# A kernel whose input test is counted at the head of its last part, read back before the last outputs, and followed directly by the block for the usual case

## The chip, the core and the metric

The program runs on one core of one Trainium2 chip. Five engines work side by side, each through its own instructions in order: TensorE (PE, with its weight loads as PEld), VectorE (DVE), ScalarE (ACT), GpSimd (POOL) and SyncE (SP), which issues all transfers here. They wait for one another through semaphores. The metric is the device time of one execution in microseconds, as a median of several runs; lower is better.

## The reference, cut to what matters

Three stages follow one another: a gated linear attention, a dense layer with a leaky activation, and a soft mixture of experts.

```python
for t in range(S):                                   # B 4, H 8, S 768, D 48
    state = alpha[:, :, t, :, None] * state + k_t outer v_t
    y[:, :, t] = q_t @ state
h = x @ w_in                                         # 3072x384 @ 384x2048
g = max(h, 0) + moe_alpha * min(h, 0)
x2 = g @ w_out                                       # 3072x2048 @ 2048x384
logits = x2 @ phi                                    # 32 slots, 4 for each of 8 experts
slot_input = softmax(logits, over tokens).T @ x2     # 32x384
slot_out[e] = max(slot_input[e] @ w1[e], 0) @ w2[e]  # 384 -> 1024 -> 384
out = softmax(logits, over slots) @ slot_out         # 3072x384
```

## The kernel before

Attention works in chunks of 128 steps and divides by products of alpha, which is safe only where alpha lies between 0.75 and 1.25; the activation is computed as a maximum of two values, which holds only where `moe_alpha` is at most 1. So the kernel carries two paths. The fast path computes everything under these assumptions and writes the output. Beside it, it keeps `flags` (a tile of 128x4x8 numbers) that tell how far alpha left its bounds. `count_ok` (L503) turns them into a count of the places where the assumptions held, `values_load` (L516) reads that count into a register of every engine, and `tc.If(ok < N_OK)` (L759) runs `general_path`, which recomputes everything step by step, if the count falls short. On the inputs timed here the assumptions hold, and the general path never runs; its instructions nevertheless stand in the program.

Each engine carries out the branch for itself. The program is laid out in blocks: the main block with the fast path, ending in the test; then the block for flags that failed (the general path); then a short block for flags that held; then the end block. The short block brings the semaphores to the values that the other block would have left: PE, DVE, ACT and POOL each wait there for their own semaphore, and SP waits for its eight transfer semaphores, so for the landing of all outputs. The end block joins the engines in two barriers.

The order of the work is written out by hand in strings: each letter is a step that issues its instructions on all engines. `START`, `STEADY` and `LAST` order attention, dense layer and token softmax; `TAIL` (L630) orders what comes after them, the part that the change touches. In it `a` transposes the sums over all tokens (`ut` on PE from `acc`, L528, then ACT's copy `uT`, L532), `b` makes the slots' inputs (`si`, L539, `sT`, L544), `c` to `f` are the first expert layer (`h`, L553), `g` to `j` its transposes, `k` to `n` the second layer (`o`, L574), `o` to `r` gather the experts' results (ACT's copy `os`, L581, and PE's `so`, L582), and `s` to `z` make the output in eight parts of 576 KB (PE L599, copies on ACT L602 and DVE L604, the transfer on SP L606). `F` loads an expert weight and `C` turns combine weights. `count_ok` is called after the whole tail.

Of the kernel before, what the change touches and what calls it, by code (L numbers as in the profile page):

```python
# [9 lines left out]
I32 = mybir.dt.int32  # L10
# [12 lines left out]
N_OK = 128 * 32  # L23
# [6 lines left out]
class Kern:  # L30
# [472 lines left out]
    def count_ok(self):  # L503
        nc = self.nc
        nc.vector.tensor_scalar(out=self.flags[:, 2:4].rearrange("p a b -> p (a b)"), in0=self.alp, scalar1=1.0, scalar2=0.0, op0=ALU.subtract, op1=ALU.max)
        ok = self.sp.tile([128, 4, NSTEP], F32, tag="ok", name="ok", bufs=1)
        nc.vector.tensor_scalar(out=ok, in0=self.flags, scalar1=0.0, scalar2=None, op0=ALU.is_le)
        oks = self.sp.tile([128, 1], F32, tag="oks", name="oks", bufs=1)
        nc.vector.reduce_sum(out=oks, in_=ok.rearrange("p a b -> p (a b)"), axis=AX.X)
        ones = self.sp.tile([128, 1], F32, tag="ones", name="ones", bufs=1)  # L510
        nc.vector.memset(ones, 1.0)
        ps = self.psa("okp")[:1, :1]
        nc.tensor.matmul(ps, oks, ones, start=True, stop=True)
        n = self.sp.tile([1, 1], I32, tag="okn", name="okn", bufs=1)
        nc.vector.tensor_copy(out=n, in_=ps)
        return nc.values_load(n, min_val=0, max_val=N_OK)  # L516

    def tail_steps(self):
        nc, sp, wt = self.nc, self.sp, self.wt
# [96 lines left out]

    def tail(self):
        steps = self.tail_steps()
        for c in TAIL:
            steps[c]()  # L620
        assert not self.queue


# [3 lines left out]
START = "lplpAxpplxABwxCpxypBpAyxlBAEpCppyDJyCBCzppyDAzFzDEJEzpGdzHCIFDpGKEHFFhGMILxOwDFGxHEhHBFhDHMgGIxgJNBIhJgHKMhLKJIhKgLxxyPyhNLhgJLNgKMNOhhLOghNhgMPyyglPPpzzypOzgNgphPhpgzgPOgphpzhg"  # L627
STEADY = "hhggsgxslhsxghhxsxgxgyhhpghhhgyysgpgpgypyzzhhhphzzsgggzgphwhg"
LAST = "hQggsxhRxxshhsTxSysggxfghsyghQzzyWhQgTyhgSyzhQQRghzRShhgUVfRghgzhThghcfggsgfShhgRWTUUhsgUhXsTgUhhgVfhVWVfWggfgVfhfghhWfXgXhgsXhXghggffhsfhfshcfgscfggSgfffsfcsfscffssfcs"
TAIL = "abFCcFdgehFfCFikFjomqFlFFvstunprxwzy"  # L630
W_ORDER = ([("w1", 4 * q + e, hf) for q in range(2) for hf in range(2) for e in range(4)]
           + [("w2", e, ch) for ch in range(2) for e in range(8)])

# [11 lines left out]
def streams(k):  # L645
    def loads():
        for c in range(3):
            k.att_load(0, ("al", "k", "q", "v"), c)
            yield
        for i in range(1, NSTEP):  # L650
            k.att_load(i, ("al", "k", "q"))
            yield

    def v_loads():
        for i in range(1, NSTEP):
            k.att_load(i, ("v",))
            yield

    def pres():
        yield from k.pre_first()  # L660
        for i in range(1, NSTEP):
            yield from k.pre_gen(i)

    def atts(c):
        for i in range(NSTEP):
            yield from k.att_chunk(i, c)

    def small():
        k.small_loads()
        yield  # L670

    def repeat(f):
        while True:
            f()
            yield

    s = {"l": loads(), "w": v_loads(), "p": pres(), "x": atts(0), "y": atts(1), "z": atts(2), "d": small(),
         "h": repeat(k.h_step), "g": repeat(k.g_step), "s": k.softs(), "f": repeat(lambda: k.feed(1)), "c": repeat(k.combine_step)}
    s.update((name, k.conv_gen(*CONV[n])) for n, name in enumerate(CONV_NAMES))
    return s  # L680


def fast_path(ctx, tc, nslots, **a):
    k = Kern(ctx, tc, a, nslots)
    k.consts()
    k.moe_init()
    s = streams(k)
    for c in START + STEADY * (NSTEP - 3) + LAST:
        next(s[c])
    k.tail()  # L690
    return k.count_ok()


def general_path(tc, nslots, ys, **a):
# [41 lines left out]
    with ExitStack() as ctx:  # L736
# [5 lines left out]
        for i in range(NSTEP):  # L742
            k.x_load(i, ys)
            k.moe_run(i)
        for _ in range(NSTEP - TAIL.count("C")):
            k.combine_step()
        k.feed(len(W_ORDER) - TAIL.count("F"))
        k.tail()


def emit(tc, nslots=26, **a):
    nc = tc.nc
    with ExitStack() as outer:
        dram = outer.enter_context(tc.tile_pool(name="ys", bufs=1, space=bass.MemoryType.DRAM))
        ys = dram.tile([768, 16, 2, 48], F32, name="ys")
        with ExitStack() as ctx:
            with tc.manual_schedule():
                ok = fast_path(ctx, tc, nslots, **a)
        with tc.If(ok < N_OK):  # L759
            general_path(tc, nslots, ys, **a)  # L760


# [53 lines left out]
```

## Time and profile before

| | |
|---|---|
| median of 3 timed runs | 542.34 us (541.62 to 544.48) |
| profiled execution, first to last instruction (span) | 540.6 us |
| PE busy | 456.7 us, 84% of the span |
| DVE busy | 411.5 us, 76% |
| ACT busy / POOL busy | 224.8 us / 139.2 us |
| mean granted TensorE clock | 0.952 |

No own time is given for the profiled execution beside its span; the median of the timed runs stands 1.7 us above it. Most of the span is dense-layer work on PE. The change lies in the last 55 us, so the reader should look at three stretches there: around 486 us, where the tail begins; around 521 us, between the two halves of the output; and from 527.7 us, where the last output copy ends, to 540.6 us.

### The profile page before, as it was taken

The page shows a single profiled execution, that of the slowest core. Times are in us where ns is not written, and L with a number is a line of the kernel's source. Part 1 is how long each engine was busy: PE and PEld are TensorE (multiplying, and loading weights), DVE is VectorE, ACT ScalarE, POOL GpSimd, SP SyncE. Part 2 cuts the span into 40 slices and gives each one's busy share as a digit, 9 for nine tenths or more (in the row PEclk, how much of TensorE's full clock was granted, in tenths as well). Part 3 has the DMA queues.
Part 4 walks back from the last instruction along what each step waited for, and adds up shares of the span by engine and source line. Part 5 has one row for each costly group of instructions (what it writes and reads, how often), then busy time and mean ns, then how long its engine had stood idle before and what let it go on. Part 6 is the DMA issues. An engine that isn't in the chain of part 4 may idle for free.

```text
span 540.6 us, 10837 instructions
## 1 busy us (share of the span) xinstructions
PE 456.7 (84%) x4316; PEld 360.1 (67%) x4316; DVE 411.5 (76%) x791; ACT 224.8 (42%) x420; POOL 139.2 (26%) x75
## 2 busy tenths in 40 slices
PE   3643588789799899989998997999899999978980
PEld 2431477777688678768786886787667887653570
DVE  6999999999577976987697789769777897662140
ACT  2755345664254334324524432443236366342140
POOL 1247575875200400220030004002202263320000
PEclk9997787899899999989999999999899999989995
DMA  8994111041202436425461724454464588989955
GB/s 298 420 403 181 58 59 59 15 162 61 116 1 52 127 74 219 96 82 117 180 172 37 246 55 133 96 198 118 140 201 188 132 329 279 373 343 389 383 193 169
DMA packets 42236, 93.99 MB, mean 174 GB/s; under 512 B 5056, under 2 KB 29888, under 8 KB 42176
## 3 DMA queue, kind: packets, MB, share of 16 engines
q1 hardware_dynamic: 42176, 93.20, 51.1%
q8 instruction: 36, 0.59, 0.4%
q14 instruction: 24, 0.20, 0.1%
HBM read 69.59 MB, written 4.72 MB: 137 GB/s over the span
## 4 chain that ended last, share of the span: by engine, by line
PE 47%; DVE 41%; ACT 5%; issue 4%; DMA 1%; SPq 0%; DVEq 0%; ACTq 0%
PE h L325 25%; DVE P L191 4%; DVE tmp L235 3%; DVE g L335 3%; PE lg L370 3%; DVE st L355 3%; DVE al L199 3%; DVE w_in L106 3%; DVE w_t L106 3%; PE sc L220 2%; DVE S L255 2%; PE o L574 2%; PE h L553 2%; DVE w_t L105 2%; ACT P L147 2%
## 5 line engine op out<-in xcount | busy, mean ns | idle before, releaser
L325 PE MATMUL h<-xh,wi 128*128 128x384 f32 x768 | 223.4, 358 | 16.0 <-ACT xh L499 9.8
L325 PEld LDWEIGHTS h<-xh,wi 128*128 128x128 f32 x768 | 146.2, 196 | 30.2 <-ACT xh L499 11.3
L325 PE MATMUL h<-xl,wi 128*128 128x384 f32 x384 | 134.1, 349 | 12.1 <-DVE xl L500 12.1
L334 ACT ACTIVATE tn<-h,alp 128x384 f32<-128x384 f32 x128 | 73.6, 581 | 128.6 <-PE h L325 112.5
L335 DVE TENSOR_TENSOR g<-h,tn 128x384 f32<-128x384 f32 x128 | 68.2, 549 | 65.7 <-ACT tn L334 61.8
L325 PEld LDWEIGHTS h<-xl,wi 128*128 128x128 f32 x384 | 75.4, 196 | 14.7 <-DVE xl L500 13.9
L193 POOL TENSOR_TENSOR q<-q,P 128x1536 f32<-128x1536 f32 x7 | 24.8, 3543 | 199.0 <-DMA gT<-st 113.2
L355 DVE STREAM_TRANSPOSE st<-g 128x192 f32<-128x192 f32 x192 | 57.0, 346 | 0.3
L220 PE MATMUL sc<-q,k 48*128 48x128 f32 x384 | 35.0, 316 | 0.0
L220 PEld LDWEIGHTS sc<-q,k 48*128 48x128 f32 x384 | 27.5, 209 | 9.0 <-issue 8.4
L268 PE MATMUL y<-tmp,v 128*32 128x128 f32 x384 | 23.2, 299 | 11.0 <-DVE tmp L235 8.1
L259 ACT COPY S<-S 64x256 f32<-64x256 f32 x20 | 8.1, 406 | 54.9 <-DVE S L255 49.8
L235 DVE TENSOR_TENSOR tmp<-sc,cst 128x512 f32<-128x512 f32 x48 | 30.6, 678 | 0.2
L370 PE MATMUL lg<-g,wpr 128*32 128x384 f32 x256 | 29.0, 506 | 0.0
L111 POOL TENSOR_TENSOR raw_w_out<-raw_w_out 128x768 f32<-128x768 f32 x8 | 12.4, 1556 | 54.8 <-PE y L281 34.1
L199 DVE TENSOR_TENSOR_SCAN al<-al,Z 128x1536 f32<-128x1536 f32 x7 | 24.7, 3530 | 0.2
L191 DVE TENSOR_TENSOR_SCAN P<-al,Z 128x1536 f32<-128x1536 f32 x7 | 24.7, 3526 | 0.0
L226 PE MATMUL kt<-cst,k 128*128 128x128 f32 x80 | 15.4, 323 | 10.1 <-DVE k L171 8.7
L268 PEld LDWEIGHTS y<-tmp,v 128*32 128x32 f32 x384 | 10.3, 113 | 20.2 <-DVE tmp L235 9.3
L348 PE MATMUL tr<-cst,g 128*128 128x128 f32 x96 | 16.2, 283 | 8.7 <-DVE g L335 6.5
L203 POOL TENSOR_TENSOR k<-k,al 128x1536 f32<-128x1536 f32 x6 | 17.4, 2907 | 22.1 <-issue 14.8
L111 POOL TENSOR_TENSOR raw_w_in<-raw_w_in 128x768 f32<-128x768 f32 x8 | 14.1, 1766 | 32.6 <-DVE raw_w_in L107 27.0
(150 smaller groups left out, 721.1 us busy)
## 6 DMA issues: line engine op xcount, KB each, us to landing
w<-w SPq DMA_DIRECT2D x32, 768.0 KB, 8.4
gT<-st SPq DMA_DIRECT2D x192, 96.0 KB, 2.2
raw_w_in<-w_in SPq DMA_DIRECT2D x8, 768.0 KB, 8.4
raw_w_t<-w_t SPq DMA_DIRECT2D x8, 768.0 KB, 9.6
raw_w_out<-w_out SPq DMA_DIRECT2D x8, 768.0 KB, 5.9
v<-vT SPq DMA_DIRECT2D x7, 768.0 KB, 4.5
al<-alT SPq DMA_DIRECT2D x7, 768.0 KB, 4.5
k<-kT SPq DMA_DIRECT2D x7, 768.0 KB, 5.9
```

Of the source, the lines that this page charges most:

```text
L106: nc.vector.scalar_tensor_tensor(out=Ai, in0=pi, scalar=-0x80000000, in1=Ai, op0=ALU.bitwise_and, op1=ALU.bitwise_or)
L111: nc.gpsimd.tensor_tensor(out=B, in0=B, in1=p, op=ALU.mult)
L191: nc.vector.tensor_tensor_scan(P, al[:, 0:W6], Z, 0.0, ALU.mult, ALU.add)
L199: nc.vector.tensor_tensor_scan(G[:, ::-1], G[:, ::-1], Z[:, ::-1], 0.0, ALU.mult, ALU.add)
L220: nc.tensor.matmul(sc[h][:, p], K[r, p, c], Q[r, p, c], start=True, stop=True)
L235: nc.vector.tensor_tensor(out=m, in0=sc[h], in1=self.tri[:, None, :].to_broadcast([128, NP, 128]), op=ALU.mult)
L268: nc.tensor.matmul(y[32 * g:32 * g + 32, kt], V[:, c, p, 0, h, :], sm[h][:, p], start=True, stop=(S is None))
L325: nc.tensor.matmul(h, w[ft // 2][:, kt, fs], x[:, kt], start=(n == 0), stop=(n == 8))
L334: nc.scalar.activation(out=t, in_=h, func=AF.Copy, scale=al)
L335: nc.vector.tensor_tensor(out=g, in0=h, in1=t, op=ALU.max)
L355: nc.vector.transpose(out=self.stage[z].rearrange("p t a f j -> p (t a) f j")[:, :, f], in_=g4[:, :, z])
L370: nc.tensor.matmul(self.lg[32 * jj:32 * jj + 32], self.wpr[:, 4 * fb + jj], self.g[4 * fb + jj], start=(fb == 0), stop=(fb == 3))
```

## The change

`count_ok` no longer returns a value: it leaves its count in a tile, and a second function `read_ok` reads it into the registers. Both become steps of the tail, `1` as its first and `2` between `p` and `r`, five steps from the end. `tc.If` is told that the block for the failed flags is not the one to follow the test, so the short block for flags that held stands directly behind it.

```diff
         ps = self.psa("okp")[:1, :1]
         nc.tensor.matmul(ps, oks, ones, start=True, stop=True)
-        n = self.sp.tile([1, 1], I32, tag="okn", name="okn", bufs=1)
-        nc.vector.tensor_copy(out=n, in_=ps)
-        return nc.values_load(n, min_val=0, max_val=N_OK)
+        self.okn = self.sp.tile([1, 1], I32, tag="okn", name="okn", bufs=1)
+        nc.vector.tensor_copy(out=self.okn, in_=ps)
+
+    def read_ok(self):
+        self.ok = self.nc.values_load(self.okn, min_val=0, max_val=N_OK)
...
         steps = self.tail_steps()
+        if not self.general:
+            steps.update({"1": self.count_ok, "2": self.read_ok})
         for c in TAIL:
-            steps[c]()
+            if c in steps:
+                steps[c]()
...
-TAIL = "abFCcFdgehFfCFikFjomqFlFFvstunprxwzy"
+TAIL = "1abFCcFdgehFfCFikFjomqFlFFvstunp2rxwzy"
...
     k.tail()
-    return k.count_ok()
+    return k.ok
...
-        with tc.If(ok < N_OK):
+        with tc.If(ok < N_OK, preferred_fallthrough_block=False):
```

Three places show what this moves. The first is PE's queue at the head of the tail; names are out<-in, and the brackets name the engines whose semaphores the instruction waits for. Before:

```order
L462 MATMUL ct<-cst,cr 128x128 [waits DVE_49,Pool_49]
L462 MATMUL ct<-cst,cr 128x128 x2
L528 MATMUL ut<-cst,acc 128x128 [waits DVE_49]
L528 MATMUL ut<-cst,acc 128x128 x3
L539 MATMUL si<-w_out_4217,uT 32x384 [waits DVE_49,Activation_49]
```

PE's queue at the same place in the changed kernel (its lines stand two further on):

```order
L462 MATMUL ct<-cst,cr 128x128 [waits DVE_49,Pool_49]
L462 MATMUL ct<-cst,cr 128x128 x2
L513 MATMUL okp<-ones,oks 1x1 [waits DVE_49,PE_49]
L530 MATMUL ut<-cst,acc 128x128 [waits Activation_49]
L530 MATMUL ut<-cst,acc 128x128 x3
```

The count's matmul now stands ahead of the transposes `ut`. What it waits for is DVE's `oks` and `ones`, whose place in DVE's queue in the changed kernel is this:

```order
L441 SCALAR_TENSOR_TENSOR acc<-acc,sc,u 128x512 [waits PE_49]
L465 TENSOR_TENSOR cs_4978<-ct,cs_4978 64x384 [waits Activation_49]
L444 TENSOR_REDUCE cd<-ce 128x3
L445 TENSOR_SCALAR cd<-cd 128x3 [waits DVE_49]
L446 RECIPROCAL cd<-cd 128x3 [waits DVE_49]
L447 TENSOR_TENSOR c<-ce,cd 128x96 [waits DVE_49]
L505 TENSOR_SCALAR flags<-alp 128x16
L507 TENSOR_SCALAR ok<-flags 128x32 [waits DVE_49]
L509 TENSOR_REDUCE oks<-ok 128x1 [waits DVE_49]
L511 MEMSET ones 128x1
L515 CAST okn<-okp 1x1 [waits PE_49]
```

Before, `rd` (L524) stood directly behind `c`, and the last five of these rows stood at the very end of the queue. Between `acc`, which `ut` reads, and `ones`, which PE now awaits first, stand eight instructions.

The second place is PE's queue between the two gathers, in the changed kernel:

```order
L576 MATMUL o_5425<-w_6_1_5365,ht_5238 32x192
L576 MATMUL o_5425<-w_7_1_5367,ht_5238 32x192
L584 MATMUL so<-os,reps 128x192 [waits Activation_49]
L518 TENSOR_LOAD okn [waits DVE_49]
L584 MATMUL so<-os,reps 128x192 [waits Activation_49]
L601 MATMUL o<-ss,cs_4470 128x192 [waits DVE_49,Activation_49]
```

The register read moved from the end of the queue to between the two `so` matmuls; on the other engines it lies in the corresponding place.

The third is SP's queue at the end of the tail. Before:

```order
L606 DMA out<-ot_2_5400 128x6x192 [waits DMAHW7_49,DVE_49,Activation_49]
L606 DMA out<-ot_1_5458 128x6x192 [waits DMAHW0_49,DVE_49,Activation_49]
L606 DMA out<-ot_0_5472 128x6x192 [waits DMAHW1_49,DVE_49,Activation_49]
L606 DMA out<-ot_3_5486 128x6x192 [waits DMAHW2_49,DVE_49,Activation_49]
L606 DMA out<-ot_2_5500 128x6x192 [waits DMAHW3_49,DVE_49,Activation_49]
L516 TENSOR_LOAD okn [waits DVE_49]
L516 ISA x2
L759 COMPARE_AND_BRANCH
```

SP's queue at the end of the tail in the changed kernel:

```order
L608 DMA out<-ot_2_5411 128x6x192 [waits DMAHW7_49,DVE_49,Activation_49]
L518 TENSOR_LOAD okn [waits DVE_49]
L518 ISA x2
L608 DMA out<-ot_1_5483 128x6x192 [waits DMAHW0_49,DVE_49,Activation_49]
L608 DMA out<-ot_0_5497 128x6x192 [waits DMAHW1_49,DVE_49,Activation_49]
L608 DMA out<-ot_3_5511 128x6x192 [waits DMAHW2_49,DVE_49,Activation_49]
L608 DMA out<-ot_2_5525 128x6x192 [waits DMAHW3_49,DVE_49,Activation_49]
L764 COMPARE_AND_BRANCH
L764 UNCONDITIONAL_BRANCH [waits DMAHW0_49,DMAHW1_49,DMAHW2_49,DMAHW3_49,DMAHW4_49,DMAHW5_49,DMAHW6_49,DMAHW7_49]
```

The last row stands for the short block: its eight waits and its branch to the end block. Before, it was the last row of SP's whole queue, 785 rows behind the test and next to the end block; now it follows the test, and the 784 rows of the other block lie between it and the end block. The same holds on the other engines.

## Rows read from the trace of the kernel before

**Rows 1.** The page: span, and code fetches (packets, MB, share).

```profile
span 540.6 us, 10837 instructions
...
q8 instruction: 36, 0.59, 0.4%
q14 instruction: 24, 0.20, 0.1%
```

**Rows 2.** Chain of waits, head of the tail: start us, us, what.

```profile
486.16 0.76 DVE acc L441
...
486.96 0.67 PE ut L528 x4
...
488.29 2.83 PE si L539 x32
```

**Rows 3.** Timeline of PE around 486 us: start us, us, what.

```profile
486.03 0.55 PE L462 MATMUL ct<-cst,cr 128*128 128x128 f32 x3
```

**Rows 4.** Chain of waits from 500 us to the end, by line.

```profile
by line: PE o L574 24.4%; PE h L553 9.8%; PE o L599 8.9%; DVE ot L604 5.3%; PE so L582 4.8%; PE hTp L564 3.6%; issue 1.8%; PE ct L462 1.1%; DVE ss L587 1.0%; ACT os L581 0.7%; ACT ss L585 0.7%; PE okp L513 0.5%; DVE ok L507 0.4%; DVE oks L5
```

**Rows 5.** Timeline of DVE around 488 us.

```profile
488.59 0.14 DVE L524 TENSOR_SCALAR rd<-den 128x1 f32<-128x1 f32 x1
```

**Rows 6.** Timeline from 514 us: second gather, count ([idle before <-releaser]).

```profile
521.85 0.32 ACT L581 COPY os<-o 128x192 f32<-128x192 f32 x1 [2.35 <-PE o L574]
...
523.25 0.73 DVE L587 TENSOR_TENSOR ss<-so,ss 32x192 fp32r<-32x192 f32 x2 [3.59 <-ACT ss L585]
...
527.74 0.17 DVE L505 TENSOR_SCALAR flags<-alp 128x16 f32<-128x16 f32 x1
...
528.42 0.19 PE L513 MATMUL okp<-ones,oks 128*1 128x1 f32 x2 [1.39 <-DVE ones L511]
```

**Rows 7.** By stretch: busy PE, PEld, DVE, ACT, POOL; granted clock, DMA share, GB/s.

```profile
478.50:481.90 3.40, 0.81 (x15) 0.63 (x19) 2.46 (x8) 1.60 (x5) 0.00 (x0) 1.00 1.02 416
482.00:485.30 3.30, 3.30 (x72) 3.30 (x65) 1.77 (x8) 0.28 (x1) 0.00 (x0) 0.50 0.72 268
485.40:488.70 3.30, 2.24 (x39) 1.38 (x35) 2.19 (x7) 1.06 (x2) 0.00 (x0) 1.00 0.81 290
```

**Rows 8.** Line L516, the register read: durations in ns, first and last start.

```profile
L516 PEldq TENSOR_LOAD <-okn x1: 1167/1167/1167, 528.8 to 528.8; - x1
```

**Rows 9.** Line L462: PE's sequencer reaches the transpose `ct`.

```profile
L462 PEldq EVENT_SEMAPHORE  x2: 51/51/51, 485.1 to 491.8; - x2
```

**Rows 10.** Line L606: output transfers, issue to landing, min/median/max.

```profile
L606 SPq DMA_DIRECT2D out<-ot x8: 372/732/1435, 517.5 to 528.1; - x8
...
DMA to landing us min/median/max: 3.3/5.2/7.3
```

**Rows 11.** Line L759: the test, then the short block.

```profile
L759 SPq EVENT_SEMAPHORE  x8: 17/17/17, 537.2 to 537.7; - x8
L759 ACTq COMPARE_BRANCH  x1: 50/50/50, 530.0 to 530.0; - x1
...
L759 PEldq COMPARE_BRANCH  x1: 6582/6582/6582, 530.1 to 530.1; - x1
...
L759 ACTq EVENT_SEMAPHORE  x1: 17/17/17, 537.1 to 537.1; - x1
```

**Rows 12.** Busy and transfers by stretch at the end.

```profile
533.50:534.00 0.50, 0.00 (x0) 0.00 (x0) 0.00 (x0) 0.00 (x0) 0.00 (x0) 0.50 0.91 293
...
537.50:538.00 0.50, 0.00 (x0) 0.00 (x0) 0.00 (x0) 0.00 (x0) 0.00 (x0) 0.50 0.36 98
```

**Rows 13.** Line L813: the end block.

```profile
L813 SPq EVENT_SEMAPHORE  x10: 17/28/28, 537.8 to 540.5; - x10
...
L813 ACTq DRAIN  x2: 8/32/56, 537.2 to 540.3; - x2
...
L813 DVEq EVENT_SEMAPHORE  x2: 21/21/21, 538.5 to 540.5; - x2
...
L813 ACTq EVENT_SEMAPHORE  x2: 17/17/17, 540.2 to 540.5; - x2
```

## The prediction

> **What bounds the kernel now.** I read the page first [rows 1], then the chain of waits around the tail's head and from 500 us on [rows 2, 4], then the timelines of single engines there [rows 3, 5, 6], and last the lines of the test and of the end block [rows 11, 13], because nothing computes in the last 12 us. The reader is to see three things.
>
> At the head, PE and the engines beside it form one chain: `acc` on DVE ends at 486.9, `ut` follows at 486.96, and `si` at 488.29 [rows 2]. From 500 us on the chain is nearly all matmuls and their copies; no transfer appears in what the row shows [rows 4]. So whatever comes late at 487 us comes late at the last output copy, which ends at about 527.7, where `flags` begins [rows 6].
>
> Then come transfers. The last output is issued at 528.1 and lands up to 7.3 us later, at 535.4 [rows 10]. The outputs still move 293 GB/s just before 534 us [rows 12].
>
> Then comes code. ACT's test stands at 530.0 and takes 0.05 us, but its next instruction, in the short block, starts only at 537.1; PE's test is recorded as 6.58 us long [rows 11]. The jump goes past the whole other block, and its code arrives only when the outputs have left. The same is to be seen once more: ACT's `DRAIN` is at 537.2 and its next wait at 540.2, though DVE passes the same barrier at 538.5 [rows 13]. Meanwhile 98 GB/s for 0.5 us, 49 KB, move [rows 12]; fetches are 16.4 KB each on one queue (0.59 MB in 36) and 8.3 KB on the other [rows 1], so this is about one 16.4 KB fetch and four of 8.3 KB, five engines. A fetch with nothing in its way therefore costs about 3.0 us from need to resumption.
>
> **The change part by part.**
>
> *The count at the head.* PE works in order, so `ut` now waits behind `okp`, and `okp` for DVE's `ones`. DVE reaches `flags` where `rd` began, 488.59 [rows 5]; from `flags` to `okp` it took 527.74 to 528.42, 0.68 us [rows 6]. So `okp` starts at 489.27 and `ut` about 0.06 later, at 489.33, against 486.96 [rows 3]: +2.4 us. Behind it on PE stands the entire tail, and ACT (`uT`), then DVE and SP wait for that. Bounds: above 2.6, with all of `okp`'s 0.19 added; below 0, if a later wait took it up, for which the chain has no candidate [rows 4], so I take 2.4. The weight loads are no cover, since they are not what the tail waits for [rows 4]. The CAST behind `okp` delays `rd`, which `sis` needs some 3 us later and so doesn't feel.
>
> *The clock.* PE ends `ct` at 486.58 [rows 3] and would now idle until 489.3. [...]
>
> *The read moved.* It takes 1.17 us on PE [rows 8]. On ACT it stands where the engine idles 2.35 us, and on DVE 3.59 [rows 6], so it costs nothing there, nor on POOL, which has finished its work, nor on SP, whose next transfer waits for DVE's copies behind `ss`. On PE it is hidden if the sequencer runs ahead of the array: it passed the wait of `ct` at 485.1 [rows 9], 0.9 us before the matmul at 486.03 [rows 3]. Read that way it would start 0.9 before the second gather, and `so` awaits ACT's `os`, which ends at 522.17 [rows 6]. Bounds: 0 to 1.2; I take 0, nearest to the 0.9. If that cover went, it would cost up to the whole 1.2.
>
> *The ending.* What falls away at the end (five DVE operations, the read, the jump to the short block) lay beside the landing outputs. What matters is what comes after the landing. SP now passes the test without a jump, and waits in the short block for its outputs. On the clock of before: landing 535.4; four more semaphores at 0.07 (eight took 537.2 to 537.7 [rows 11]), 0.3; then the jump past the other block, 3.0; then the end block, from SP's first wait at 537.8 to the barrier passed at 538.5 [rows 13], 0.7, and to the end without ACT's late arrival another 0.6, an estimate. Sum 540.0 against 540.6: -0.6. If the five fetches no longer share the engines with the last output, it lands when the stream runs dry, at about 534.5, and it is -1.5. I take -0.8, close to the measured landing; the bounds are -1.5 and, with the ending as long as before, 0.
>
> [...]
>
> *Sum:* +2.4 + 1.0 + 0 - 0.8 = +2.6 us on the span of 540.6, so 543.2. The timed median stands 1.7 us above that span, and I carry this over: 542.3 + 2.6 = 544.9 us, 0.5% more at the most. Changes under 0.5%, 2.7 us, can't be told from none here (the bounds are 539.6 and 545.1), so the forecast is "no change", close to its upper edge.
>
> **The rivals.**
>
> *PE holds its queue at the read* until the matmuls before it have drained. Place: between the two `so`. Then it starts at 522.3 instead of about 521.0 and `so` waits 1.2 us longer: 546.1, slower. It decides from the moment when the read starts later than 521.0 on the clock of before. The wait passed 0.9 us ahead speaks against [rows 9]; no row shows a read with work queued before it.
>
> *The ending gives nothing back.* ACT's code arrives only when the outputs have left, as before [rows 12], and the end block costs it a second fetch again, 537.2 to 540.2 [rows 13]. Then the end stays at 540.6 on the clock of before: +3.4, 545.7, slower. It decides if ACT enters the end block later than 536. For it: the block is as far into ACT's code as before. Against: ACT now jumps as soon as its last copy is done.
>
> [...]
>
> *The last jump is cheap.* Nothing is queued ahead of it, and if its code is there the 3.0 shrink to 0.05: 544.9 - 3.0 = 541.9, no change, still under 542.3. Only if the clock holds too, and the output lands by 534.5, does it come near 539.9. ACT's 3.0 us with no output in flight speak against it [rows 12, 13]. [...]
>
> **How the numbers follow.** Forecast 0.42, of which 0.15 lies above 545.1; PE holds its queue 0.12; the ending gives nothing 0.16; the clock holds 0.13; the cheap jump 0.11; and 0.06 for a gain over 2.7 us that I can't derive. Slower: 0.15 + 0.12 + 0.16 = 0.43. Same: 0.27 + 0.13 + 0.11 = 0.51. Faster: 0.06. The range goes from 541.5, just below the cheap jump, to 546.7, above the held queue by half of the clock's uncertainty, and leaves out less than 2 in 10.
>
> **What would show it.** In the changed kernel's chain `ut` should start about 2.4 us later after `acc`, released by `ones`, with a stretch at 0.50 granted clock soon after; the read on PE should end before `os` of the second gather; the tests should take no time in any engine; and between SP's last wait in the short block and its first in the end block there should be a gap near 3 us. The forecast is wrong if `ut` isn't held, if the gap is missing, or if the end still follows ACT's late arrival.

## The result, and the profile after

The changed kernel takes 545.55 us (median of 9 runs, 544.71 to 549.89), the kernel before 542.34 (9 runs): a ratio of 1.0065, with an interval of 1.0044 to 1.0086, so 3.5 us slower (2.4 to 4.7; the two medians differ by 3.2). The forecast was 544.9 us and "no change". The time lies in the range, but the change is slower by a little more than the 0.5%, 2.7 us, that were to tell the two apart; its interval reaches below that line.

The profiled execution is a long one: 547.35 us, 1.8 above the median. Its span is 4.9 us longer than that of before, and 1.2 of these arise ahead of any changed instruction: `acc` ends at 488.1 us, before at 486.9 [rows 2]. So stretches are compared below, each by its own length.

The chain of waits of the changed kernel at the head (start us, us, what):

```profile
487.30 0.49 PE ct L462 x3
...
488.32 0.56 DVE cs L465
...
489.60 0.26 DVE c L447
...
490.20 0.19 DVE oks L509
...
490.54 0.19 PE okp L513 x2
490.73 0.60 PE ut L530 x4
...
491.99 4.51 PE si L541 x32
```

Before, `ut` came right behind `acc`, and DVE's `cs` and `c` stood off the chain [rows 2]. Now they stand on it, since `okp` waits for what DVE does behind them. PE's timeline shows the price in brackets:

```profile
487.23 0.55 PE L462 MATMUL ct<-cst,cr 128*128 128x128 f32 x3
490.54 0.19 PE L513 MATMUL okp<-ones,oks 128*1 128x1 f32 x2 [2.76 <-DVE ones L511]
490.66 0.66 PE L530 MATMUL ut<-cst,acc 128*128 128x128 f32 x4
```

`ut` starts 2.54 us after `acc`, before 0.05. The other thing to see is `si`: 4.51 us, before 2.83 [rows 2]. The stretches show the clock behind it (columns as in [rows 7], the granted clock third from the end):

```profile
486.10:489.40 3.30, 1.68 (x47) 1.24 (x39) 1.74 (x5) 0.48 (x1) 0.00 (x0) 1.00 0.73 281
489.60:492.90 3.30, 1.69 (x18) 0.95 (x22) 1.09 (x8) 0.58 (x1) 0.54 (x1) 1.00 0.96 371
493.00:496.30 3.30, 3.30 (x24) 0.85 (x16) 0.00 (x0) 0.00 (x0) 0.00 (x0) 0.50 1.02 388
...
527.10:530.40 3.30, 1.99 (x13) 1.45 (x13) 0.91 (x3) 1.06 (x3) 0.00 (x0) 1.00 1.07 355
530.60:533.80 3.20, 3.20 (x17) 3.19 (x15) 2.30 (x5) 1.89 (x5) 0.00 (x0) 0.50 0.71 227
```

PE is busy for half of 486.1 to 492.9, and from 493.0 on the granted clock is 0.50 instead of 1.00, in the middle of `si`. It is 0.50 again from 530.6 on, in the last output matmuls. These take 4.52 us, before 2.90:

```profile
529.50 4.52 PE L601 MATMUL o<-ss,cs 128*128 128x192 f32 x24 [1.31 <-DVE ss L589]
```

```profile
524.13 2.90 PE L599 MATMUL o<-ss,cs 128*128 128x192 f32 x24 [1.32 <-DVE ss L587]
```

Then the read, which was moved (line L518; durations in ns, first and last start):

```profile
L518 ACTq TENSOR_LOAD <-okn x1: 1122/1122/1122, 524.2 to 524.2; - x1
...
L518 PEldq TENSOR_LOAD <-okn x1: 1107/1107/1107, 526.0 to 526.0; - x1
```

PE's read ends at 527.1, before the `os` that `so` awaits (527.2 to 527.5): it is hidden. Last the test with the short block (L764), and the end block (L818):

```profile
L764 PEldq COMPARE_BRANCH  x2: 91/2694/5297, 532.1 to 534.2; - x2
L764 ACTq COMPARE_BRANCH  x2: 38/44/49, 533.6 to 534.2; - x2
...
L764 SPq COMPARE_BRANCH  x2: 42/46/49, 535.1 to 541.5; - x2
```

```profile
L818 SPq EVENT_SEMAPHORE  x10: 17/28/28, 544.1 to 545.4; - x10
...
L818 ACTq DRAIN  x2: 8/44/80, 538.3 to 545.0; - x2
```

Each engine has two branch records here, the test and the jump to the end block, and passes the test at once (0.05 to 0.09 us). The jump takes longer: PE's is recorded as 5.30 us, beside the landing outputs. ACT is in the end block at 538.3, 3.6 us after the last output's issue, before 9.1 after it [rows 10, 13]. But SP's jump past the other block, at 541.5, now stands behind the landing of the outputs, and its next instruction comes at 544.1: a gap of 2.6 us in which nothing else is left to do.

### The profile page after: what moved, and what is told of

Same layout as the page of the kernel before. It is cut to its first block, busy times and chain, and to the rows that moved or that the text cites. A ratio compares the mean times of both kernels' runs of the same rounds, so it can differ in the third digit from the quotient of the medians.

```text
span 545.5 us, 10843 instructions
## 1 busy us (share of the span) xinstructions
PE 461.7 (85%) x4316; PEld 365.3 (67%) x4316; DVE 412.1 (76%) x791; ACT 224.8 (41%) x420; POOL 138.5 (25%) x75
## 4 chain that ended last, share of the span: by engine, by line
PE 47%; DVE 40%; ACT 5%; issue 4%; DMA 1%; SPq 0%; DVEq 0%; ACTq 0%
PE h L325 25%; DVE P L191 4%; DVE tmp L235 3%; DVE g L335 3%; DVE st L355 3%; PE lg L370 3%; DVE al L199 3%; DVE w_in L106 3%; DVE w_t L106 3%; PE sc L220 2%; DVE S L255 2%; PE o L576 2%; PE h L555 2%; DVE w_t L105 2%; ACT P L147 2%
## 5 line engine op out<-in xcount | busy, mean ns | idle before, releaser
L348 PE MATMUL tr<-cst,g 128*128 128x128 f32 x96 | 17.4, 299 | 8.9 <-DVE g L335 6.7
```

## The experiments

There were twelve runs, in three groups of four with the kernel before timed beside each. Each group ran on a chip of its own. Ten runs were timed for an interval and two are of one execution; one of the ten repeats the changed kernel. This table has the lengths of the stretches in each profile in us: from the span's start to `acc`'s end, from there to the first `h`, from there to the last output's issue, and from there to the end. All come from the timelines and the issue rows. "Sum" is the last three against before, "timed" is the measured ratio to the kernel before less one, times 542.5 us, with its interval.

| kernel | to `acc` | to `h` | to issue | to end | sum | timed |
|---|---|---|---|---|---|---|
| before | 486.9 | 6.08 | 35.08 | 12.53 | | |
| before, again | 485.8 | 6.08 | 35.05 | 12.31 | -0.3 | |
| changed | 488.1 | 10.25 | 36.32 | 10.79 | +3.7 | +3.5 (2.4, 4.7) |
| changed, again | 489.7 | 11.05 | 35.07 | 11.55 | +4.0 | +5.5 (3.6, 7.4) |
| count at the head alone | 489.4 | 10.10 | 35.07 | 9.65 | +1.1 | +2.4 (1.1, 3.7) |
| layout alone | 488.4 | 6.08 | 35.04 | 11.19 | -1.4 | -1.5 (-2.8, -0.2) |
| split count, early read, new layout | 488.3 | 6.08 | 35.06 | 11.63 | -0.9 | +0.1 (-1.1, 1.2) |
| changed, PE filled | 488.1 | 8.56 | 35.07 | 11.85 | +1.8 | +2.8 (1.3, 4.3) |
| the same, again | 486.6 | 8.57 | 35.06 | 11.66 | +1.6 | |
| count one step later | 488.1 | 7.72 | 35.06 | 11.52 | +0.6 | +2.7 (1.1, 4.2) |
| split count, late read, old layout | 489.7 | 6.08 | 35.05 | 10.02 | -2.5 | -2.4 (-3.8, -1.0) |
| split count, early read, old layout | 489.4 | 6.08 | 35.07 | 9.33 | -3.2 | -2.8 (-4.1, -1.5) |
| split count, no test | 487.4 | 6.08 | 35.07 | 7.45 | -5.1 | -5.2 (-7.2, -3.1) |
| before with a hint | 485.7 | 6.08 | 35.08 | 9.00 | -3.5 | -3.6 (-4.9, -2.3) |

Where neither the clock falls nor PE is held, the two middle stretches agree within 0.04 us, so what is left to explain is the head and the ending. The first column is the same code in all and still differs by 4 us; in the three groups it goes by the group, and so by the chip (485.7 to 487.4 in the last one, 488.1 to 489.7 in the first two), not by the edit.

**Count at the head alone.** The count stays at the head, the read goes back to the end, and the blocks lie as before.

```diff
-TAIL = "1abFCcFdgehFfCFikFjomqFlFFvstunp2rxwzy"
+TAIL = "1abFCcFdgehFfCFikFjomqFlFFvstunprxwzy2"
...
-        with tc.If(ok < N_OK, preferred_fallthrough_block=False):
+        with tc.If(ok < N_OK):
```

> The count is a step at the head of the tail; the read stays at the end and the block for flags that held stays behind the other one. Theory 1 (PE's wait at the head is the loss: 2.5 us, and 1.0 to 1.7 us of lower clock behind it): 3.5 to 4.2 us over the kernel before, 545.8 to 546.5 us; ut starts about 2.5 us after acc ends, and the time from the last landing to the end stays near 5.2 us. Theory 2 (the early read or the jump that was moved is the loss): no more than 0.5 us over the kernel before.

Measured: 544.95 us, ratio 1.0045 (1.0021 to 1.0069). The head is that of the changed kernel: `okp` waits 2.75 us for `ones`, and `si` takes 3.84 us. But the time is less than theory 1 had, because the ending is shorter than in the kernel before and the changed one, 9.65 us. Its test and the short block:

```profile
L764 SPq EVENT_SEMAPHORE  x8: 17/17/17, 542.3 to 542.8; - x8
...
L764 ACTq COMPARE_BRANCH  x1: 50/50/50, 534.5 to 534.5; - x1
...
L764 SPq COMPARE_BRANCH  x1: 45/45/45, 537.5 to 537.5; - x1
...
L764 ACTq EVENT_SEMAPHORE  x1: 17/17/17, 540.1 to 540.1; - x1
```

SP tests at 537.5, and its first wait in the short block comes at 542.3; the last output, issued at 534.6, lands up to 7.5 us later, at 542.1, so the jump lies beside the landing. So the old layout, with the count out of the way, ends earlier than the new one. Neither theory had this.

**Layout alone.** The kernel before, with the one word on the test.

```diff
-        with tc.If(ok < N_OK):
+        with tc.If(ok < N_OK, preferred_fallthrough_block=False):
```

> Count and read stay at the end; only the block for flags that held is put directly behind the test. Theory 1: 0.5 to 1.5 us under the kernel before (541.4 us), since the jump moves behind the landing but ACT's second fetch goes; ut starts right after acc. Theory 2: 1 to 3 us over the kernel before.

Measured: 541.55 us, ratio 0.9973 (0.9949 to 0.9997), as expected. From issue to end it takes 11.19 us: SP's jump stands at 536.9, its next instruction at 539.4, a gap of 2.5 us. ACT enters the end block at 538.1 and keeps nobody waiting, where before SP waited for it.

**The count split.** DVE's part of the count goes one step on, PE's part and the copy behind the first `h`; read and layout are as changed.

```diff
...
+    def sum_ok(self):
+        nc = self.nc
         ps = self.psa("okp")[:1, :1]
-        nc.tensor.matmul(ps, oks, ones, start=True, stop=True)
+        nc.tensor.matmul(ps, self.oks, self.ones, start=True, stop=True)
...
-            steps.update({"1": self.count_ok, "2": self.read_ok})
+            steps.update({"1": self.count_ok, "3": self.sum_ok, "2": self.read_ok})
...
-TAIL = "1abFCcFdgehFfCFikFjomqFlFFvstunp2rxwzy"
+TAIL = "a1bFCcFd3gehFfCFikFjomqFlFFvstunp2rxwzy"
```

> The changed kernel, but with the count in two: DVE's four operations are a step behind the first (DVE idles there), the count's matmul and its copy a step behind the first two parts of the first expert layer; read and layout as in the changed kernel. Theory 1: PE no longer waits, so 0.5 to 1.5 us under the kernel before (541.4 us), 4 us under the changed kernel. Theory 2: like the changed kernel, 545 us.

Measured: 542.87 us, ratio 1.0001 (0.9979 to 1.0023). The head went as theory 1 has it: PE's timeline has no wait for `ones`, and `si` is short.

```profile
488.33 0.66 PE L533 MATMUL ut<-cst,acc 128*128 128x128 f32 x4 [0.39 <-DVE acc L441]
489.66 2.79 PE L544 MATMUL si<-w_out,uT 128*32 128x384 f32 x32 [0.67 <-ACT uT L537]
```

The ending, 11.63 us, is 0.4 longer than with the layout alone, though the count has left it, and theory 1's 541.4 is missed by 1.5 us: SP's waits for the outputs end 7.7 us after the last issue, with the layout alone after 7.3. SP's jump stands at 537.2 and its next instruction at 539.7, so in the new layout the gap of 2.5 us behind the landing is there whether the count is done early or late.

```profile
L767 SPq COMPARE_BRANCH  x2: 43/46/49, 530.8 to 537.2; - x2
```

```profile
L821 SPq EVENT_SEMAPHORE  x10: 17/28/28, 539.7 to 541.0; - x10
```

**PE filled while it waits.** 14 transposes, whose result nobody reads, stand ahead of `okp`.

```diff
         ps = self.psa("okp")[:1, :1]
+        if not self.general:
+            fill = self.psa("fill")
+            for j in range(14):
+                nc.tensor.transpose(fill[:, j % 4 * 128:(j % 4 + 1) * 128], self.ident, self.ident)
```

> The changed kernel with 14 transposes of the identity on PE just ahead of the count's matmul (0.165 us each, about 2.3 us); nothing reads them. Theory 1 with the clock as its second part: PE's wait stays, the fall of the clock behind it goes, so 1.0 to 1.7 us under the changed kernel, about 544.2 us, and si takes 2.8 us and not 4.5. If the clock falls for another reason, or not more often than before: the changed kernel's 545.5 us.

Measured: 545.43 us, ratio 1.0052 (1.0024 to 1.0079), whose interval holds theory 1's 544.2 us and the changed kernel's 545.5. The profile tells more: `okp` is as late as in the changed kernel, but `si` takes 2.79 us, as on PE's timeline in the kernel before. The kernel was profiled once more for that.

> One more look at the run with 14 transposes ahead of `okp`. Theory 1 (PE's idle stretch ahead of `okp` is what lets the clock fall behind it): `si` again takes 2.8 us, from `acc` to the first `h` 8.5 to 8.7 us, against 10.1 to 11.1 in the three profiles of the count at the head without the filling. Theory 2 (the first look was luck of where the clock's periods lay): `si` 3.8 to 4.8 us and 10 to 11 us.

Its PE timeline, and the stretches from `fill` on:

```profile
486.63 1.75 PE L515 MATMUL fill<-cst 128*128 128x128 f32 x14 [0.39 <-DVE acc L441]
489.00 0.19 PE L517 MATMUL okp<-ones,oks 128*1 128x1 f32 x2 [0.62 <-DVE ones L511]
489.11 0.66 PE L534 MATMUL ut<-cst,acc 128*128 128x128 f32 x4
490.45 2.79 PE L545 MATMUL si<-w_out,uT 128*32 128x384 f32 x32 [0.68 <-ACT uT L538]
```

```profile
485.60:488.90 3.30, 2.39 (x22) 1.82 (x17) 2.62 (x10) 0.48 (x1) 0.45 (x1) 1.00 0.96 318
489.00:492.30 3.30, 2.62 (x30) 1.30 (x34) 0.37 (x3) 0.59 (x1) 0.00 (x0) 1.00 0.97 402
492.40:495.70 3.30, 2.60 (x29) 1.38 (x25) 0.26 (x1) 1.04 (x2) 0.00 (x0) 1.00 0.85 292
```

In both filled profiles `acc` to `h` takes 8.6 us: the 6.1 of before and the 2.5 of the wait. In the three profiles with the count at the head and no filling it takes 10.1 to 11.1 and `si` 3.84 to 4.80, with a granted clock of 0.50 in stretches of the changed kernel and its repeat. In all eleven others nothing is drawn out: `acc` to `h` takes 6.08 us and what PE waits, `h` to the last issue 35.04 to 35.08. So the drawn-out `si` goes with PE's idle stretch at the head, and filling that took it away, in five profiles of five. But not every idle stretch brings one: with the count one step later, the next run here, PE idles 2.29 us in one piece and `si` behind it takes 2.79 us (491.07 to 493.86). What the filling is worth over many executions the times don't settle, since the intervals overlap.

**Count one step later.**

```diff
-TAIL = "1abFCcFdgehFfCFikFjomqFlFFvstunp2rxwzy"
+TAIL = "a1bFCcFdgehFfCFikFjomqFlFFvstunp2rxwzy"
```

> The changed kernel with the whole count one step later, so that `ut` stands ahead of `okp` on PE, and `si` behind it; read and layout as changed. Theory 1 (the cost at the head is PE's wait for DVE's `ones`, as long as `ones` is later than what PE could do otherwise): `ut` starts 0.05 us after `acc` again; `okp` still waits until about 2.5 us after `acc`, and `si`, which before stood 1.33 us after `ut`, waits until 2.6 us after `acc`: held by 1.2 us instead of 2.5, so 1.2 to 2 us below the changed kernel, ratio to before 1.002 to 1.004. Theory 2 (the cost is the count's own work on DVE, wherever it stands): as the changed kernel, 1.0065.

Measured: 545.02 us, ratio 1.0049 (1.0020 to 1.0078), 2.5 us below the changed kernel of the same group. The ratio alone can't decide, since its interval holds theory 1's 1.002 to 1.004 and theory 2's 1.0065; the profile does.

```profile
488.11 0.66 PE L530 MATMUL ut<-cst,acc 128*128 128x128 f32 x4 [0.39 <-DVE acc L441]
491.06 0.16 PE L513 MATMUL okp<-ones,oks 128*1 128x1 f32 x1 [2.29 <-DVE ones L511]
491.07 0.52 PE L541 MATMUL si<-w_out,uT 128*32 128x384 f32 x2
```

`ut` is free and `si` is held, by 1.6 us rather than 1.2: `ones` is 0.5 later, since `rd` now goes first on DVE and `flags` takes 0.49 us instead of 0.17. The cost goes with PE's wait, as theory 1 says. The matmuls of the tail are not drawn out in the profile (`si` 2.79 us, the last output matmuls 2.89), and its sum is 2.1 us under the timed loss, which I can't explain from one profile.

**Late read and old layout with the split count, and the early read there.** Two kernels that differ by the read's place alone. The edit of the first, against the kernel with the split count:

```diff
-TAIL = "a1bFCcFd3gehFfCFikFjomqFlFFvstunp2rxwzy"
+TAIL = "a1bFCcFd3gehFfCFikFjomqFlFFvstunprxwzy2"
...
-        with tc.If(ok < N_OK, preferred_fallthrough_block=False):
+        with tc.If(ok < N_OK):
```

> The count is split (DVE's part one step after the first output projection, PE's part and the copy three steps later), the read stays at the end, and the blocks lie as before. Theory 1 (a test that every engine reaches before the last output has landed lets the far jump's code come beside the landing, so the old layout then costs nothing, while in the new layout SP's far jump of 2.5 us stands behind the landing): from the last output's issue to the end about 9.6 us as in the run with the count alone at the head, instead of 12.5 before and 11.6 in the split run with the new layout; `ut` not held; time 2.5 to 3 us below the kernel before (ratio 0.9945 to 0.9954), about 2 us below the split run with the new layout. Theory 2 (code for the jump comes only when the outputs have left, whenever it is asked for, and ACT's second fetch of 3.0 us comes behind it as before): issue to end stays at 12.0 to 12.5, ratio 0.999 to 1.001.

> The split count with the read five steps ahead of the end and the old layout; it differs from the run before it in this list by the read's place alone, and from the split run of the first group by the layout alone. Theory 1 (the read is hidden at either place, the layout decides): the same time as with the late read within 0.5 us, issue to end about 9.6 us. Theory 2 (the early read on PE or SP costs something that the split run hid): 0.5 to 1.3 us above the run with the late read.

Measured: 539.63 us, ratio 0.9956 (0.9930 to 0.9982) with the late read, and 539.67, 0.9949 (0.9925 to 0.9973) with the early one: theory 1 in both. With the late read the test, the short block and the end block look like this:

```profile
L767 SPq EVENT_SEMAPHORE  x8: 17/17/17, 538.9 to 539.5; - x8
...
L767 ACTq COMPARE_BRANCH  x1: 50/50/50, 530.8 to 530.8; - x1
...
L767 SPq COMPARE_BRANCH  x1: 45/45/45, 533.8 to 533.8; - x1
L767 ACTq EVENT_SEMAPHORE  x1: 17/17/17, 535.7 to 535.7; - x1
```

```profile
L821 SPq EVENT_SEMAPHORE  x10: 17/28/28, 539.5 to 540.8; - x10
```

The last output is issued at 530.8 and lands up to 7.5 us later. ACT's code comes at 535.7, before that, and SP's at 538.9. So the code comes 4.9 and 5.1 us after these tests, is fetched beside the outputs and doesn't wait for their end, and of the far jump no more is left than the 0.6 us by which SP's code comes behind the landing at 538.3. The early read costs nothing either: 35.07 us to the issue against 35.05.

**The changed kernel again.** The same kernel, on the chip of the last three kernels.

> The changed kernel once more, on the chip of the three others, so that they can be compared with it directly: ratio 1.0044 to 1.0086 by its first runs. In its profile the head's wait is again 2.5 us; if the loss by the clock depends on where its periods fall in an execution, the falls behind `ut` and in the last output matmuls need not both be there again.

Measured: 547.55 us, ratio 1.0101 (1.0066 to 1.0136), of six executions. That is more than the expected 1.0044 to 1.0086, though the intervals overlap. The head repeats; the drawn-out last output matmuls don't, with 2.89 us after 4.52.

```profile
492.16 0.19 PE L513 MATMUL okp<-ones,oks 128*1 128x1 f32 x2 [2.76 <-DVE ones L511]
492.28 1.11 PE L530 MATMUL ut<-cst,acc 128*128 128x128 f32 x4
494.07 4.80 PE L541 MATMUL si<-w_out,uT 128*32 128x384 f32 x32 [0.67 <-ACT uT L534]
```

Here `ut` is slow too, 1.11 us; two stretches in a row have a granted clock of 0.50:

```profile
491.40:494.70 3.30, 1.86 (x10) 1.02 (x14) 0.92 (x8) 0.58 (x1) 0.54 (x1) 0.50 1.00 384
494.80:498.20 3.40, 3.40 (x28) 1.09 (x24) 0.00 (x0) 0.00 (x0) 0.00 (x0) 0.50 0.87 272
```

The ending, without the drawn-out outputs of the first profile, is 11.55 us.

**No test.** The split count and the early read, without the test and the general path. The edit, against the kernel with the split count:

```diff
-        with tc.If(ok < N_OK, preferred_fallthrough_block=False):
-            general_path(tc, nslots, ys, **a)
```

> The split count with the early read and without the test and the general path behind it (the kernel leaves out the general path, so it has no jump past it at the end). Theory 1 (what is left of the ending in the run with the split count, the early read and the old layout is the landing of the outputs and the closing barriers, since the jump's code comes beside the landing there): from the last output's issue to the end 8.7 to 9.3 us, against 9.33 in that run; ratio to before 0.993 to 0.995. Theory 2 (code fetches still delay the outputs or SP there by more than half a microsecond): 7.5 to 8.3 us, ratio 0.991 to 0.9925.

Measured: 537.56 us, ratio 0.9905 (0.9868 to 0.9942): theory 2, a little past its range. Theory 1 had nothing left but the landing and the barriers, and was 1.3 us off. The last stretches of this kernel show when the outputs are through; below them stand those of the kernel before:

```profile
533.20:534.90 1.70, 0.00 (x0) 0.00 (x0) 0.00 (x0) 0.00 (x0) 0.00 (x0) 0.50 0.71 222
534.90:535.90 1.00, 0.00 (x0) 0.00 (x0) 0.00 (x0) 0.00 (x0) 0.00 (x0) 0.50 0.00 0
```

```profile
534.00:534.50 0.50, 0.00 (x0) 0.00 (x0) 0.00 (x0) 0.00 (x0) 0.00 (x0) 0.50 0.29 97
534.50:535.00 0.50, 0.00 (x0) 0.00 (x0) 0.00 (x0) 0.00 (x0) 0.00 (x0) 0.50 0.00 0
```

The last issue stands at 528.5, so nothing moves any more 6.4 us after it; in the kernel before, with its last issue at 528.1, nothing moves 6.4 us after it either. So the outputs' data are not through sooner. What is shorter is the whole ending, 7.45 us against 9.33 with the test, and whether the code of the test holds up the landing or SP in these 1.9 us, no run separates.

**The kernel before with a hint.** Late count, late read, old layout; the engines are told that the branch will be taken.

```diff
+        self.tc.mark_branch_hint_location("okif", hint="LikelyTaken", engines=list(mybir.ALL_ENGINES))
         return nc.values_load(n, min_val=0, max_val=N_OK)
...
-        with tc.If(ok < N_OK):
+        with tc.If(ok < N_OK, label="okif"):
```

> The kernel before with a hint to the engines that the test's branch will be taken; nothing else differs, and the hint stands at the head of the program. Theory 1 (the ending of before is long because the short block's code is fetched beside the outputs, and the hint makes it be there): the short block begins within 1 us of the test on ACT and PE instead of 7, issue to end falls from 12.5 to 9.5 to 10, 2.5 to 3 us below before, ratio 0.9945 to 0.9954. Theory 2 (a hint given so far ahead is lost by the time of the test): as before, ratio 0.998 to 1.002, the test on PE again 6 to 7 us long.

Measured: 539.27 us, ratio 0.9933 (0.9909 to 0.9958): theory 1, and a little more. The test and the short block, the hint, and the end block:

```profile
L760 PEldq COMPARE_BRANCH  x1: 398/398/398, 528.9 to 528.9; - x1
...
L760 ACTq EVENT_SEMAPHORE  x1: 17/17/17, 529.2 to 529.2; - x1
```

```profile
L814 PEldq BRANCH_PREFETCH_HINT  x1: 50/50/50, 0.8 to 0.8; - x1
```

```profile
L814 SPq EVENT_SEMAPHORE  x10: 17/28/28, 534.5 to 535.8; - x10
```

PE's test takes 0.40 us instead of 6.58 [rows 11], and the short block begins 0.4 us after ACT's test at 528.8 instead of 7.1. With the late count left in place, the ending is the shortest of all kernels with a test: it was the code that made it long, not the count.

**The kernel before again.** One execution.

> One more look at the kernel before, for the stretches that the change doesn't touch. From `acc` to the first `h` 6.1 us, from there to the last output's issue 35.1, and from that issue to the end 12.3 to 12.7, as in its first profile. The end of `acc` stood at 486.9 us there and at 488.1 to 489.7 in the profiles of the nine other kernels: if executions differ there by themselves it lies anywhere from 486.5 to 490, if the other kernels are really later there, at 486.9 again.

Measured: 541.0 us in one execution. `acc` ends at 485.8, below both expectations; the other stretches are those of the first profile, within 0.2 us. That the first column differs between profiles of the same code is shown; what sets it, the chip or the execution, is open.

## Why the prediction was right or wrong

*The count at the head*, +2.4: right. `ut` waits 2.49 us more behind `acc` in the profile after, and with the count split it waits no more.

*The clock*, +1.0 in the sum: no run shows this term; it was an estimate of mine, and too small. What the runs show reads from the stretch `acc` to `h`, less 6.08 and less what `ut` was held more than before: 1.7 us after, 2.5 in the repeat, 1.3 with the count at the head alone. In the profile after, the output matmuls add another 1.2. A stretch at 0.50 behind the wait came as expected in the profile after and in the repeat. But its start differed, from 0.9 us ahead of `ut` in the repeat to 2.3 us behind its start in the profile after, where it fell on 3.3 us of solid matmuls; and in the repeat a second one followed, so that `ut` and nearly all of `si` lie in the two. The 0.50 at 530.6 us was not thought of; one profile of two has it, so it is no steady cost.

*The read moved*, 0: right, by the row of PE's read and by the pair that differs in nothing else.

*The ending*, -0.8: right in size, 12.3 to 12.5 us before and 11.55 in the repeat; the 10.79 of the first profile come from outputs that were drawn out ahead of the last issue, so that SP's waits end 6.8 us after it, in the repeat 7.6. The jump of 2.6 us behind the landing was forecast as 3.0. What was wrong is a sentence ahead of it, that the code comes only when the outputs have left. It comes beside them, in some 5 us, where it is asked for early. (In the kernel before, all five engines also ask within 1.1 us, from 530.0 to 531.1; with the split count, the late read and the old layout POOL asks at 502.0 and the others from 530.4 to 533.8. How much of the difference that makes, no run separates.) SP tests 3.0 us after the last issue in the kernel before and in the one with the split count, the late read and the old layout alike; but there ACT tests at that issue instead of 1.9 us behind it, and the closing barriers no longer wait for it: from SP's first wait in the end block to the end 1.3 us, before 2.8 [rows 13]. SP's test in the kernel before:

```profile
L759 SPq COMPARE_BRANCH  x1: 45/45/45, 531.1 to 531.1; - x1
```

So I missed that the two halves of the change work against each other: with the count out of the way the old layout ends after 9.3 to 10.0 us, and the new one puts SP's far jump behind its waits, 11.5 to 11.9.

Behind SP's waits for the outputs, its next instruction comes 2.5 to 2.6 us after its far jump in the traces (537.2 to 539.7 with the split count, the early read and the new layout, 541.5 to 544.1 in the changed kernel). In the old layout with the early count the same wait lay beside the landing outputs, and that decided here.

*The sum.* The terms as measured are 2.5 for the wait, 1.3 to 2.5 for the clock and -0.8 to -1.0 for the ending, +2.8 to +4.2, around the timed +3.5. The forecast was low by the clock's share. The repeat's 547.55 us, with 2.5 for the clock, even lies above the forecast's range, which ended at 546.7.

*The rivals.* PE didn't hold its queue at the read, which ended at 527.1, ahead of `os` at 527.5. The ending did give something back, ACT being early. The clock did not hold, with 0.50 in the profile after and in the repeat, and `si` drawn out to 3.84 us with the count at the head alone. The last jump wasn't cheap, with 2.5 to 2.6 us; what a hint made cheap is the test's branch in the old layout, and the hint was not part of the change.

## What to carry to other kernels

A small matmul that is put in early must find its operands ready: what stood behind it on PE here paid its wait in full, 2.5 us, and in the three profiles where PE idled for it another 1.3 to 2.5 of drawn-out matmuls. Move the part that waits (here DVE's sum) and the part that others queue behind (the matmul) to different places. At a far branch look which engine takes it last and what it could have waited for meanwhile: behind the landing outputs the far jump cost 2.5 us here, and beside them the test with all its code cost 1.9 (9.33 us from issue to end, 7.45 without). A hint on the branch alone gave as much as the best reordering that keeps the test (3.6 and 2.8 us, with intervals that overlap).

## What was not expected of the hardware

With a hint given at 0.8 us of the span PE's branch at 528.9 took 0.40 us, without it 6.58. Without the test the ending took 7.45 us, with it 9.00 at the least, though the outputs' data were through no sooner, 6.4 us after the last issue as before. And the same instructions up to `acc` end anywhere from 485.7 to 489.7 us, as much as the whole effect of this change, so single profiles are to be compared by stretches and not by spans.
